# f32 parameter tables kept in DRAM, powers and weights made per channel quarter in that quarter's own Z buffer, two power tables, 112 quads instead of 107

## The chip, the core and the metric

The kernel runs on one core of a Trainium2 chip. The core has five engines, each with its own instruction stream: TensorE (PE, matmuls; PEld is its weight loads), VectorE (DVE), ScalarE (ACT), GpSimd (POOL) and SyncE (SP), whose queue issues nearly all DMAs here. The metric is the device time of one execution, in microseconds.

## The reference

The inputs are bf16: `x` (1 x 2048 x 512), attention weights, and the parameters of a diagonal state-space model with 512 channels and 128 complex states each.

```python
g = sigmoid((x * gate_w).sum(-1))
# branch a: attention, 32 heads of 16 channels, full softmax over 2048 keys
p = softmax(q @ k.T * 16 ** -0.5); a = (p @ v) @ wo
# branch b: y[l] = sum_m K[d, m] u[l - m], u = x
logdA = exp(log_dt) * (A_re + 1j * A_im)
K[d, l] = Re(sum_n C[d, n] * exp(logdA[d, n] * l) * dt * B[d, n])      # l = 0 .. 2047
b = causal_convolution(K, x) + x * Dskip
out = g * a + (1 - g) * b
```

The largest single job is the exponential: 32 heads x 2048 x 2048 scores, 134 million of them.

## The kernel before, in words

**Attention.** The work is cut into 2048 tiles of 128 keys x 512 queries for one head. A block is four heads with one of the four query chunks: there are 32, of 64 tiles each, and a quad is the four tiles of a block's four heads that share a key tile. A group takes three tiles: `qk(g)` writes their scores into one of two PSUM buffers of 3 x 512 columns (`SC0`, `SC1`), `ex(g)` (L987) makes one ACT exponential over 1536 columns into the ring `ET`/`EX`, and `pv` sums them against V into the PSUM bank `OA`, with a column of ones for the denominator. There are 683 groups.

**Quads on DVE and POOL.** Not all tiles go to ACT. `decide` (L865) may take a whole quad out: its four tiles become the third tile of four groups, whose ACT instruction then covers 1024 columns. For the third tile `bits` (L1010) has DVE write a 16-bit linear approximation of the exponential's bit pattern (`DZ`, L1014); when a quad's four tiles are there, `batch` has POOL make three shifted copies by an integer addition (`DU`, L1028, three per quad), and `sums` adds `DZ` and the three `DU` on TensorE. Before, 107 quads are handled so. `PACE` (L60) is a table of group number and number of quads that may have begun by then, `WIN` says which buffers are used in which groups.

**Kernel of the state-space branch.** `params` and `params2` (L1127, L1144) compute on DVE, in f32 and for all 512 channels at once, the powers L1, L2, ..., L64 of exp(logdA), the inverse powers M1 to M8, and the weights WW = C dt B and WN. From these, for each quarter of 128 channels:

- `powers` (L1221) makes 16 powers of each channel in a table `B16`, working in the f32 scratch `FP`;
- `weights` (L1181) makes the first 8 columns of `Z` in the same scratch;
- `zpart` (L1301) multiplies these out to the 32 columns of `Z`;
- `tables` makes, for each of a quarter's four channel blocks, the table `T` from `B16` and the digit table `DT` (four DVE products of 1536 columns at L1397, plus a copy by DMA);
- `kstage` (L1408) multiplies `T` by `Z` on TensorE into the PSUM bank `MB` and stores the block's kernel to DRAM (`kd`).

Before, `bases` (L1336) makes powers and weights of quarters 1, 2 and 3 ahead, in the staging buffers `B16s` and `Zbs`, and stores them to the DRAM scratch `bd`; quarter 0 is made in place once that is done (`TGO = 'bw31'`), and `tables` loads the other quarters back when their turn comes. There is one `B16` buffer (`NB = 1`) and two `Z` buffers (`NZ = 2`), used by the quarters in turn.

**Convolution and output.** `yloads` and `ystage` (L1503) convolve with Toeplitz slices of `kd` (`H`) and of x (`U`) on TensorE in `MB`, DVE scales and stores them (`Yst`, L1531), and `outs` (L1620) projects the attention with Wo, adds the convolution and writes the 16 row tiles of the output: 0 to 11 while attention runs, through `MB` and DVE (`fo`, L1652 and L1656), 12 to 15 after the last group.

**Fillers.** TensorE also multiplies a tile of zeros (`wm`) into a bank in use: L981 does it once in each even group, and the loop at L1812 adds as many as are needed for `FILL` units of array work per group.

**What sets the order.** The program is written out once, by a planner that runs when the kernel is built. The main loop (L1775) places each group's exponential and score matmuls; all else is threads with a priority, each a sequence of segments on one engine with a planned cost. `Sched.fill` picks the segment that could start first, then the one with the lower priority number. So constants such as `PACE`, `FILL`, `LAZY` or a priority change the order of the whole program. On the chip each engine runs its list in order and waits on semaphores.

## Time and profile before

| | us |
|---|---|
| median of 3 runs | 772.46 (772.38 to 777.15) |
| the profiled execution | 771.4 |
| its span in the profile | 769.6 |
| ACT busy | 745.3 (97%) |
| PE busy | 692.1 (90%) |
| DVE busy | 643.4 (84%) |
| POOL busy | 344.7 (45%) |

The durations below are those of the one profiled execution. Its own time is 1.8 us longer than its span, and 1.1 us under the median. In rows of groups of instructions the columns are: line, engine, operation, output<-input with shapes, count | busy us, mean ns of one | idle us of the engine before them and what ended it. Successive ACT instructions overlap by some 0.3 us in the records, so an ACT instruction's mean is longer than the distance between two starts.

### The profile page before, as it was taken

To read this page: it belongs to the slowest core of one execution; us is meant where nothing else is said; L and a number is where in the kernel's file an instruction comes from. 1 tells how busy PE (TensorE), PEld (TensorE's weight loads), DVE (VectorE), ACT (ScalarE), POOL (GpSimd) and SP (SyncE) were. 2 spreads that over 40 slices of the span, in tenths; PEclk is the share of its full clock that TensorE was granted. 3 is DMA by queue.
4 is the path that set the end of the run, shared out by engine and by line. 5 is a ranking of instruction groups with operands and counts; after the bars stand their busy time and mean duration, and the time that the engine had idled before them with its cause. 6 is when DMAs were issued, how large, how long until landed. Compare 5 with 4: busy or idle time off the path is not lost.

```text
span 769.6 us, 31882 instructions
## 1 busy us (share of the span) xinstructions
PE 692.1 (90%) x14179; PEld 291.5 (38%) x14180; DVE 643.4 (84%) x1069; ACT 745.3 (97%) x694; POOL 344.7 (45%) x340
## 2 busy tenths in 40 slices
PE   7777888787898899999999998999999999999996
PEld 3222332221344445443445444544443444422222
DVE  7999999999986998889998898877877566787883
ACT  7999999999999999999999999999999999999992
POOL 5000000010243464464655654545787555777771
PEclk9999999999999999999999999999999999999999
DMA  9459112212057665746645568356868999710001
GB/s 200 80 101 115 43 63 97 95 64 61 18 127 177 167 174 137 199 98 169 164 106 160 150 156 220 87 132 157 205 158 186 193 201 193 162 29 24 24 16 55
DMA packets 168427, 95.54 MB, mean 124 GB/s; under 512 B 117729, under 2 KB 148834, under 8 KB 167906
## 3 DMA queue, kind: packets, MB, share of 16 engines
q1 hardware_dynamic: 166274, 92.33, 51.4%
q8 instruction: 111, 1.82, 1.0%
q10 hardware_dynamic: 2016, 1.18, 0.7%
q14 instruction: 26, 0.21, 0.1%
HBM read 63.81 MB, written 19.42 MB: 108 GB/s over the span
## 4 chain that ended last, share of the span: by engine, by line
ACT 86%; PE 9%; DVE 2%; DMA 1%; issue 1%; ACTq 0%; POOL 0%; DVEq 0%
ACT ET L992 79%; ACT EX L992 7%; PE SC L734 4%; PE OA L734 3%; PE MB L734 2%; DMA Wk<-in_A_wqkv_dram 1%; DVE DZ L1014 1%; DVE T L1073 1%; DVE fo L1656 0%; ACTq L738 0%; DVE ft L1073 0%; DVE Z L1073 0%; POOL DU L1028 0%; ACT fo L1856 0%; DVE OT L1049 0%
## 5 line engine op out<-in xcount | busy, mean ns | idle before, releaser
L992 ACT ACTIVATE ET<-SC 128x1024 bf16<-128x1024 f32 (+1 forms) x615 | 679.5, 1380 | 4.0 <-PE SC L734 1.6
L1028 POOL INT64_ADD DU<-DZ x321 | 333.7, 1053 | 389.7 <-DVE B L1256 136.0
L1014 DVE TENSOR_SCALAR DZ<-SC 128x512 uint16<-128x512 f32 x428 | 287.5, 685 | 75.9 <-PE SC L734 70.9
L734 PE MATMUL SC<-Qm,KT 32*128 32x512 bf16 x2048 | 271.9, 384 | 59.9 <-ACT ET L992 54.0
L734 PEld LDWEIGHTS SC<-Qm,KT 32*128 32x128 bf16 x2048 | 69.5, 91 | 259.7 <-ACT ET L992 203.4
L734 PE MATMUL OA<-ET,VE 128*32 128x512 bf16 x1478 | 150.1, 387 | 1.7 <-DVE OT L1049 0.8
L734 PE MATMUL OA<-wm 32*128 32x512 bf16 (+3 forms) x721 | 148.7, 351 | 1.2 <-DVE idf L784 1.2
L734 PE MATMUL OA<-DU,VE 128*32 128x512 bf16 x1284 | 125.7, 386 | 0.6 <-POOL DU L1028 0.4
L734 PEld LDWEIGHTS MB<-U,H 128*32 128x32 bf16 x4096 | 85.7, 143 | 26.8 <-issue 14.9
L734 PE MATMUL MB<-U,H 128*32 128x128 bf16 (+7 forms) x4096 | 91.6, 224 | 0.6 <-DVE DZ L1014 0.6
L992 ACT ACTIVATE EX<-SC 128x1024 bf16<-128x1024 f32 (+1 forms) x68 | 73.0, 1290 | 0.0
L1073 DVE TENSOR_TENSOR T<-B,DT 128x1536 bf16<-128x1536 bf16 x64 | 65.3, 1054 | 0.0
L734 PEld LDWEIGHTS OA<-ET,VE 128*32 128x32 bf16 x1478 | 38.9, 95 | 59.9 <-issue 54.5
L734 PEld LDWEIGHTS OA<-DU,VE 128*32 128x32 bf16 x1284 | 34.0, 96 | 42.7 <-issue 34.2
L734 PEld LDWEIGHTS MB<-T,Z 128*32 128x32 bf16 x2048 | 44.6, 154 | 12.9 <-issue 8.8
L734 PE MATMUL MB<-T,Z 128*32 128x48 bf16 (+1 forms) x2048 | 48.4, 235 | 0.2 <-issue 0.2
L734 PE MATMUL OA<-DZ,VE 128*32 128x512 bf16 x428 | 42.3, 385 | 0.0
L734 PEld LDWEIGHTS OA<-wm 128*32 128x32 bf16 (+2 forms) x721 | 38.3, 94 | 10.5 <-issue 8.3
L1531 DVE TENSOR_TENSOR Yst<-MB,gt 128x512 bf16<-128x512 f32 x32 | 22.0, 686 | 18.4 <-PE MB L734 17.9
L1049 DVE STREAM_TRANSPOSE OT<-OA 128x512 f32<-128x512 f32 x32 | 22.7, 709 | 3.0 <-PE OA L734 3.0
L1073 DVE TENSOR_TENSOR ft<-Z,DM 128x1024 bf16<-128x1024 bf16 x32 | 23.6, 756 | 0.0
L734 PE MATMUL MB<-Wv,xT 128*32 128x128 bf16 x1024 | 19.9, 220 | 0.7 <-DVE VE L838 0.5
(143 smaller groups left out, 438.1 us busy)
## 6 DMA issues: line engine op xcount, KB each, us to landing
H<-gm_kd SPq DMA_DIRECT2D x128, 256.0 KB, 4.0
U<-gm_xs SPq DMA_DIRECT2D x128, 134.2 KB, 3.8
T<-B SPq DMA_DIRECT2D x16, 256.0 KB, 2.9
gm_yd<-Yst SPq DMA_DIRECT2D x64, 64.0 KB, 2.9
gm_bd<-B16s SPq DMA_DIRECT2D x3, 1024.0 KB, 4.9
B<-gm_bd SPq DMA_DIRECT2D x12, 256.0 KB, 3.6
gm_kd<-Ks SPq DMA_DIRECT2D x64, 40.0 KB, 2.6
gm_xs<-xP SPq DMA_DIRECT2D x16, 136.0 KB, 7.3
```

What stands on the lines that cost most here:

```text
L734: op("PE", lambda t: t.matmul(out(), lhsT(), rhs(), start=start, stop=stop, skip_group_check=True, **kw), R, W, c=c, lat=.15, a=a, cfg=cfg)
L992: op("ACT", lambda a: a.activation(E(at, [[1, 512 * n]]), sc(0, [[1, 512 * n]]), AF.Exp, scale=DH ** -0.5), [(sc, i, g) for i in range(n)] ...
L1014: op("DVE", lambda v: v.tensor_scalar(z.u16(512 * k, [[1, 512]]), sc(1024, [[1, 512]]), XS, XB, ALU.mult, ALU.add), [(sc, 2, g)], [(z, k, ...
L1028: op("POOL", lambda v, u=u, cut=cut: v.int64_add(u.u64(), z.u64(), cut * 0x0001000100010001), R, [(u, 0, i)], c=1.016, lat=.09, lk=True)
L1049: op("DVE", lambda v: v.transpose(OT(512 * w, [[1, 512]]), OA(0, [[1, 512]])), [(OA, 0, b)], [(OT, w, b)], c=.64)
L1073: op(eng, lambda v: v.tensor_tensor(o(), a(), b_(), f), R, W, c=c)
L1531: op("DVE", lambda v, w=w, h=h: v.tensor_tensor(Yst(1024 * w + 4 * h, [[128, R8], [8, 16], [1, 4]]), MB(0, [[1, R8], [R8, 16], [NC, 4]]), ...
```

## The change

The f32 results `L1, L2, L4, L8, M2, M4, WW, WN` are stored to a DRAM scratch `pd`, laid out by quarter (`park`, 16 DMAs of 256 KB). `ploads` loads a quarter's eight tables into that quarter's Z buffer, seen as f32 (4 DMAs per quarter, 1 MB in all), once the Z buffer's earlier quarter is done with (`KT3`, `KT7`). `powers` and `weights` then work inside the Z buffer, with its later bf16 columns as their scratch; `zpart` writes over them last. The scratch `FP`, the staging buffers and the way through `bd` go, and so do the 20 copies into `FP`. There are two `B16` buffers. `DT` is split by quarter, so `short` for the three digit tables becomes `digit`: 24 instructions for 6. The thread that made the tables is split into `bases` (powers, weights, `zpart`) and `tables` (`T`).

With that go new planner constants: a new `PACE`, other waits for starting threads (`XGO`, `TGO`), `outs` at priority 1 in place of 6, and `ZEND = 230`: from group 230 on no filler matmuls are issued. In the program as built 112 quads are taken instead of 107, the fillers `OA<-wm` of 128 columns by 512 fall from 313 to 117, those of 32 by 512 from 172 to 72.

```diff
-LAZY = 9
-PDEL = .2
+LAZY = 8
+PDEL = 0.1
+ZEND = 230
+OUTP = 1
-OVER = .3
+OVER = 0.4
-PACE = ((0, 0), (110, 0), (170, 4.8), (230, 16.2), (300, 28.8), (370, 42.8), (440, 54.0), (510, 70.1), (560, 79.1), (620, 93.5), (683, 108.6))
+PACE = ((0, 0), (40, 0), (90, 0.0), (140, 0.0), (200, 9.0), (270, 24.4), (340, 41.2), (420, 58.8), (500, 74.8), (570, 88.8), (630, 102.6), (683, 112.67))
-XGO = 'g14'
+XGO = 'g30'
-TGO = 'bw31'
-BPR = 2
-KP = 0.20
-NB = 1
+TGO = 'g0'
+TP = 2
+KP = 0.4
+NB = 2
...
-    sb("DT", 3 * 6 * D)
+    for k in range(4):
+        sb(f"DT{k}", 3 * 6 * P)
-    sb("FP", 2 * 128 * 8, FP32)
-    sb("B16s", 2 * 128 * 16)
-    sb("Zbs", 2 * 128 * 8)
...
-            if i == 0 and n == 3 and g % 2 == 0 and sch.now is not None:
+            if i == 0 and n == 3 and g % 2 == 0 and g < ZEND and sch.now is not None:
...
+    def digit(n):
+        m, x = DIGITS.index(n), B[n]
+        for qr in range(4):
+            d = B[f"DT{qr}"]
+            yield ("DVE", .45)
+            op("DVE", lambda v, d=d, qr=qr: v.tensor_copy(d(6 * P * m, [[2 * P, 2], [2, P], [1, 2]]), x(P * qr, [[D, 2], [1, P], [0, 2]])), [(x, 0)], [(d, (m, 0))], c=.07 + .28)
+            op("DVE", lambda v, d=d, qr=qr: v.tensor_scalar(d(6 * P * m + 4 * P, [[2, P], [1, 2]]), x(D + P * qr, [[1, P], [0, 2]]), -1.0, None, ALU.mult), [(x, 0)], [(d, (m, 1))], c=.07 + .14)
+        sch.mark("D" + n)
...
-        for l, n in enumerate(("WW", "WN")):
-            yield ("DVE", .25)
-            op("DVE", lambda v, l=l, n=n: v.tensor_copy(FP(128 * l, [[e8, 2], [1, 128]]), B[n](d0, [[D, 2], [1, 128]])), key(n), rw(l), c=.25)
...
-        yield from copy(1, "L1")
-        yield from copy(2, "L2")
-        yield from copy(4, "L4")
...
+    def park():
+        for n in ("L1", "L2", "L4", "L8", "M2", "M4", "WW", "WN"):
+            yield ("AFTER", n)
+            k = PDS.index(n)
+            for h in range(2):
+                yield ("SP", .6)
+                dma("SP", lambda e, k=k, n=n, h=h: e.dma_start(pd.dram(1024 * h + 128 * k, [[8192, P], [2048, 4], [1, 128]]), B[n](D * h, [[128, 4], [1, 128]])),
+                    key(n), [(pd, (n, h))], c=.6, lat=4, b=.65)
+        sch.mark("pd")
+
+    def ploads():
+        yield ("AFTER", "pd")
+        for qr in range(4):
+            Z = B[f"Z{qr % NZ}"]
+            if qr >= NZ:
+                yield ("AFTER", f"KT{4 * (qr - NZ) + 3}")
+            for k0, n, over, at in ((0, 2, [3, 5], 256), (2, 2, [(1, 0), (1, 1)], 640), (4, 1, [(0, 0), (0, 1)], 1024), (5, 3, [(2, 0), (2, 1)], 1536)):
+                yield ("SP", .6)
...
+    def bases():
         yield ("AFTER", TGO)
         for qr in range(4):
+            if qr >= NB:
+                yield ("AFTER", f"T{4 * (qr - NB) + 3}")
+            yield from powers(qr, B16, [(B16, 0), (B16, 2)])
+            yield from weights(qr)
             yield ("AFTER", "DM9")
             yield from zpart(qr)
+            sch.mark(f"ba{qr}")
...
-                   (tables(), 2), (bases(), BPR), (xrows(), 4), (outs(), 6)):
+                   (tables(), TP), (bases(), 2), (park(), 2), (ploads(), 2), (xrows(), 4), (outs(), OUTP)):
...
-        sch.fill(t, t + OVER, want)
-        lack = want - p.act
+        sch.fill(t, t + OVER, want if g < ZEND else 0)
+        lack = want - p.act if g < ZEND else 0
```

How the order moves is shown at three places.

**The end, on TensorE.** From the last two score tiles (`SC<-Qm,KT` x2, group 682) up to the output projection of tiles 13 to 15. `OA<-DU` and `OA<-DZ` are the sums of the last quads, `OA<-ET` and `OA<-EX` those of ACT's tiles, `MB<-Wo,OnR` with the two `MB<-Yl` one output tile of the first twelve, `MB<-Wo,OnT` tile 12. Before:

```order
L734 MATMUL SC<-Qm,KT 128x512 x2
L734 MATMUL OA<-DZ_65,VE 32x512 x4
L734 MATMUL MB<-Wo,OnR_75 32x512 x8
...
L734 MATMUL OA<-DU_70,VE 32x512 x4
L734 MATMUL MB<-Yl,idb 32x512 x4
L734 MATMUL MB<-Yl_102,idb 32x512 x4
L734 MATMUL OA<-DU_71,VE 32x512 x4
L734 MATMUL MB<-Wo,OnR_75 32x512 x16
...
L734 MATMUL MB<-Wo,OnT_72 32x512 x12
```

Now:

```order
L740 MATMUL OA<-DZ_62,VE 32x512 x4
L740 MATMUL MB<-Wo,OnR_75 32x512 x8
L740 MATMUL MB<-Yl,idb 32x512 x4
L740 MATMUL SC<-Qm,KT 128x512 x2
L740 MATMUL OA<-ET,VE 32x512 x4
L740 MATMUL OA<-DU_66,VE 32x512 x4
L740 MATMUL MB<-Yl_102,idb 32x512 x4
L740 MATMUL OA<-DU_67,VE 32x512 x4
L740 MATMUL OA<-ET,VE 32x512 x4
L740 MATMUL OA<-DU_68,VE 32x512 x4
L740 MATMUL MB<-Wo,OnT_72 32x512 x12
```

Before, output tiles 9, 10 and 11 stand behind the last score tiles (the shown lines of 8 and 16 and, among those left out, 4, 4 and another 16); now only the last step of tile 11 does, the second `Yl`. The last quad has moved up as well: its last DZ is read ahead of the last score tiles, not behind.

**The end, on DVE.** From the last quad's conversions (`DZ`) on; `CAST fo<-MB` is the evacuation of one output tile, `OT<-OA` the transpose of a finished block. Before:

```order
L1014 TENSOR_SCALAR DZ_64<-SC 128x512 x4
L1014 TENSOR_SCALAR DZ_65<-SC 128x512 x4
L1656 CAST fo<-MB 128x512 x4
L1049 STREAM_TRANSPOSE OT<-OA 128x512
L1057 RECIPROCAL Rz<-OT 128x16
```

Now:

```order
L1070 TENSOR_TENSOR ON<-OT,Rz 128x16x16
L1671 CAST fo<-MB 128x512
L1020 TENSOR_SCALAR DZ_62<-SC 128x512 x3
L1671 CAST fo<-MB 128x512
L1020 TENSOR_SCALAR DZ_62<-SC 128x512
L1671 CAST fo<-MB 128x512
L1055 STREAM_TRANSPOSE OT<-OA 128x512
```

Before, four evacuations stand behind the last conversion; now one.

**The quarters' powers, on DVE.** A stretch of quarter 2's part, which before stands ahead of the first conversion of a quad (`FP` scratch, staging buffer `B16s`):

```order
L1206 COPY FP<-WN 128x2x128
L829 CAST KT<-MB 128x512
L1073 TENSOR_TENSOR ft_146<-FP,M_134 128x512
L1073 TENSOR_TENSOR ft_147<-FP,M_134 128x512
L1189 CAST Zbs<-FP 128x256
L1073 TENSOR_TENSOR FP<-ft_146,ft_147 128x256
```

Now a like stretch for quarter 3, near the end of its weights, in the Z buffer itself:

```order
L1218 CAST Z_153<-Z_153 128x256
L1079 TENSOR_TENSOR Z_153<-ft_148,ft_149 128x512
L1020 TENSOR_SCALAR DZ_56<-SC 128x512
L1079 TENSOR_TENSOR Z_153<-ft_148,ft_149 128x512
L1546 TENSOR_TENSOR Yst<-MB,gt 128x128x4
L1020 TENSOR_SCALAR DZ_56<-SC 128x512 x2
```

Before, the powers and weights of quarters 1, 2 and 3 and most of quarter 0's powers stand ahead of the first conversion. Now those of quarters 0 and 1 do, with about half of quarter 2's powers; the rest of quarter 2 and quarter 3 stand between the quads. Ahead of the first conversion stand now also the `zpart` of quarters 0 and 1, 29 of the 64 products for `T` and the transposes and casts of six of the sixteen `kstage`; before, none of these. In all DVE has 297 instructions ahead of it before and 357 now. The first conversion belongs to group 112 before, to group 141 now.

## The prediction

> **What bounds the kernel now.** I read the page first: which engine is full, and which one the chain of work that ended last runs through.

> ```profile
> span 769.6 us, 31882 instructions
> PE 692.1 (90%) x14179; PEld 291.5 (38%) x14180; DVE 643.4 (84%) x1069; ACT 745.3 (97%) x694; POOL 344.7 (45%) x340
> PEclk9999999999999999999999999999999999999999
> ACT 86%; PE 9%; DVE 2%; DMA 1%; issue 1%; ACTq 0%; POOL 0%; DVEq 0%
> ```

> ACT works 97% of the span and is 86% of the chain, so a change pays by what it takes off ACT, or off the stretches in which ACT has nothing to do. The groups by form say what one exponential costs, ACT's waits how long it stood still between them.

> ```profile
> L992 ACT ACTIVATE ET<-SC 128x1024 bf16<-128x1024 f32 x367 | 356.2, 1184 | 2.1 <-PE SC L734 1.3
> L992 ACT ACTIVATE ET<-SC 128x1536 bf16<-128x1536 f32 x248 | 346.0, 1672 | 1.9 <-PE OA L734 1.5 <-PE SC L734 0.4
> ACT ET L992 <- PE SC L734: 1.6, 5, 0.5
> ACT ET L992 <- PE OA L734: 1.5, 2, 1.3
> ```

> Busy time by count is 346.0/248 = 1.395 us for the wide form and 356.2/367 = 0.971 us for the narrow one: 0.424 us for 512 columns. (The means 1672 and 1184 ns overlap their neighbours; busy time counts overlap once.) Between the exponentials ACT lost only 1.6 + 1.5 = 3.1 us. Its one large gap is at the end, so I read the timeline there, engine by engine.

> ```profile
> 749.74 3.78 ACT L992 ACTIVATE EX<-SC 128x1024 bf16<-128x1024 f32 x3
> 765.27 1.07 ACT L1856 CAST fo<-SC 128x512 bf16<-128x512 f32 x2 [11.75 <-PE SC L734]
> 749.76 0.69 DVE L1014 TENSOR_SCALAR DZ<-SC 128x512 uint16<-128x512 f32 x1 [0.23 <-PE SC L734]
> 750.37 0.68 DVE L1656 CAST fo<-MB 128x512 bf16<-128x512 f32 x1
> 753.96 0.69 DVE L1656 CAST fo<-MB 128x512 bf16<-128x512 f32 x1 [2.91 <-PE MB L734]
> 758.87 0.69 DVE L1656 CAST fo<-MB 128x512 bf16<-128x512 f32 x1 [1.76 <-PE MB L734]
> 754.80 1.05 PE L734 MATMUL MB<-Wo,OnR 128*32 128x512 bf16 x16 [0.52 <-DVE fo L1656]
> 755.66 0.65 PE L734 MATMUL MB<-Yl,idb 128*32 128x512 bf16 x8
> 759.62 0.83 PE L734 MATMUL MB<-Wo,OnT 128*32 128x512 bf16 x12 [0.86 <-DVE fo L1656]
> 761.09 0.59 PE L734 MATMUL SC<-Wo,OnT 128*128 128x512 bf16 x2 [0.16 <-issue]
> 761.61 0.40 PE L734 MATMUL OA<-EX,VE 128*32 128x512 bf16 x4
> ```

> The exponentials end at 765.27 - 11.75 = 753.5. The sums over the last of them (`OA<-EX`) start at 761.61, 8.1 us later: PE first builds output tiles 9, 10 and 11, each of which needs the one bank `MB` and so waits for DVE's evacuation of the tile before. From 761.61 to the end of the span it is 8.0 us, a chain of small steps that the change leaves alone.

> **The change part by part.**

> *Five quads more.* Each takes four tiles from ACT: 20 x 0.424 = 8.5 us off an engine that hardly waits. DVE and POOL pay:

> ```profile
> L1014 DVE TENSOR_SCALAR DZ<-SC 128x512 uint16<-128x512 f32 x428 | 287.5, 685 | 75.9 <-PE SC L734 70.9 <-PE OA L734 2.1 <-POOL DU L1028 1.5
> L1028 POOL INT64_ADD DU<-DZ x321 | 333.7, 1053 | 389.7 <-DVE B L1256 136.0
> L1234 DVE COPY FP<-L 128x256 f32<-128x256 f32 x12 | 3.4, 282 | 0.0
> L1120 DVE CAST DT<-L 128x2048 bf16<-128x2048 f32 x3 | 3.6, 1217 | 0.0
> L1124 DVE TENSOR_SCALAR DT<-L 128x1024 bf16<-128x1024 f32 x3 | 2.0, 682 | 0.0
> L1120 DVE CAST DL<-L 128x512 bf16<-128x512 f32 x1 | 0.4, 421 | 0.0
> ```

> DVE gets 20 x 287.5/428 = 13.4 us, POOL 15 x 1.053 = 15.8 us. The 20 copies into `FP`, each of 256 columns, save 20 x 0.282 = 5.6 us. The digit tables took 3.6 + 2.0 = 5.6 us; now 12 casts at `DL`'s 0.421 and 12 products of 256 columns at the copy's 0.282 make 8.4, so +2.8. DVE is left with 13.4 - 5.6 + 2.8 = +10.6: 654 us of a span of some 756, 87%. POOL comes to 344.7 + 15.8 = 361, under half. Neither becomes the bound on the whole.

> *Does DVE fit stage by stage?* Work moves ahead of the first conversion, and ACT cannot pass a conversion that is late: its third tile holds the score bank that the group after next needs.

> ```profile
> 20.00:160.00 140.00, 111.53 (x2179) 40.25 (x2171) 134.30 (x254) 140.00 (x107) 1.20 (x5) 1.00 0.43 86
> 160.00:760.00 600.00, 559.18 (x11748) 242.01 (x11748) 490.01 (x772) 589.80 (x574) 333.65 (x321) 1.00 0.55 131
> L1014 DVE TENSOR_SCALAR DZ<-SC x428: 626/691/847, 162.5 to 749.8; 128x512 uint16<-128x512 f32 x143
> L1073 DVE TENSOR_TENSOR T<-B,DT 128x1536 bf16<-128x1536 bf16 x64 | 65.3, 1054 | 0.0
> L1073 DVE TENSOR_TENSOR ft<-Z,DM 128x1024 bf16<-128x1024 bf16 x32 | 23.6, 756 | 0.0
> L1437 DVE STREAM_TRANSPOSE Kt<-MB 128x512 f32<-128x512 f32 x16 | 11.4, 711 | 4.5 <-PE MB L734 4.4
> L1440 DVE CAST Ks<-Kt 128x512 bf16<-128x512 f32 x16 | 7.3, 455 | 0.5
> ```

> (The windows' columns are length, then busy of PE, PEld, DVE, ACT, POOL, then the granted clock.) Up to the first conversion, at 162.5, DVE is nearly full: 134.3 of 140 us. Ahead of it now stand 29 `T` products (29 x 65.3/64 = 29.6), 36 of `zpart` (36 x 0.756 = 27.2), six blocks' `Kt` with their three casts (6 x (0.711 + 0.455) = 7.0, and the 12 small casts at the copy's 0.282 at most 3.4), four evacuations more at 0.69 (2.8) and the digits' 2.8. Against that, 33 instructions of powers and weights fewer, by the window's mean of 134.30/254 = 0.529 us, are -17.5, and 18 of the copies -5.1: together +50.2 by durations. Durations overlap: the conversion at 749.76 lasts 0.69, its successor starts 0.61 later. For 60 instructions more that is 60 x 0.08 = 4.8 less, +45. The first conversion belongs to a group 29 later; the wide form's 1.395 makes 40.5 us of that, and 5.7 us were idle: 46. It just fits, with some 5 us of error either way; 5 us too late costs ACT 5 us, once. After it DVE has 490.0 + 10.6 - 45 = 456 us in 600 - 40.5 - 14 = 545, 84%, beside 490.0 of 600, 82%, before.

> I take the waits between exponentials from 3.1 to 4.1 us, **+1.0**. The bounds are -3.1 (all gone) and +10: 5 at the front, and 5 where a conversion stands behind a f32 power of quarters 2 or 3.

> Those powers read two SBUF inputs beside POOL's additions, where before they stood ahead of them. The `T` products already did: 65.3/64 = 1.02 us each beside POOL, 0.07 from the mean that overlap leaves, so the row holds the price of it, and I add nothing.

> [...]

> *The way through DRAM.* Sixteen stores of 256 KB and sixteen loads on SP's queue take the place of 6 and 18.

> ```profile
> gm_bd<-B16s SPq DMA_DIRECT2D x3, 1024.0 KB, 4.9
> 29.22 11.11 SPq L1464 DMA_TRANSPOSE xP<-in_A_x_dram  x8
> 46.23 3.07 SPq L848 DMA_DIRECT2D Qm<-gm_qd  x4
> 58.64 0.68 DVE L1073 TENSOR_TENSOR WN<-pt,pt 128x512 f32<-128x512 f32 x1
> 74.89 1.22 DVE L1120 CAST DT<-L 128x2048 bf16<-128x2048 f32 x1
> ```

> An issue takes 3.07/4 = 0.77 us, a transpose 11.11/8 = 1.4. The sixteen stores are 12 us of SP ahead of what it did there: the transposes of x, which only the convolution reads, and the `Qm` loads for the third block, which starts near 70 (43 groups of 1.395 after a start near 12), 20 us after they were made. The last store waits for `WN`, done at 59.3. Even with all seven transposes that stand near it behind that, the two stores and the first three loads are issued by 59.3 + 9.8 + 3.9 = 73 and land 4.9 later, by 78. The first power that reads them stands behind the last digit cast and its product, which begin at 74.89 before and end near 78 with the digits' 2.8. So it is just hidden; without that, DVE idles and it is the late front above. Quarters 2 and 3 load when `KT3` and `KT7` free their buffer; behind the waiting load on SP is the very `Ks` store that follows the same block, so no one else waits. I put it at nothing.

> *The end.* On PE only the second `Yl` of tile 11 stands behind the last score tiles; tile 12's Wo can start about when the exponentials end. From there to the last sums it is 761.61 - 759.62 = 2.0 us by the rows above: 8.1 - 2.0 = **6.1 us** less. Bounds: 0, if evacuations still chain behind the last conversions, and 7.6, if tile 12 is done by then and only its last 0.5 is left. The three tiles' matmuls do not vanish; they move in among the score matmuls, 3 x (1.05 + 0.65) = 5 us, hidden by PE's waits for ACT:

> ```profile
> PE SC L734 <- ACT ET L992: 59.1, 175, 1.0
> 282.00:740.00 458.00, 436.83 (x9320) 192.08 (x9311) 371.41 (x583) 455.01 (x453) 279.72 (x272) 1.00 0.60 142
> 282.00:740.00 458.00, 80.64 (x275) 19.64 (x275) 0.00 (x0) 1.00 0.60 142
> ```

> *No fillers from group 230.* The first window is all work from there on, the second the zero products `wm` alone: 80.6 of PE's 436.8 us go, and PE is left with 356/458 = 78%. On the path they are nothing, since PE waits for ACT anyway. What they might hold up is the clock, a rival below.

> **Sum.** 771.4 - 8.5 - 6.1 + 1.0 = 757.8 for the profiled execution; the median of the runs is 1.1 above it: **759.0**.

> **The rivals.**

> *Half the gain is eaten.* The plan is dense: DVE at 83 to 87% in order, PE with output steps between score matmuls. If the front is late by the full 5 and mid conversions by 5 (+10 in place of +1), it is 768. If only the end stays as it was, 765. For: the front fits with nothing to spare. Against: 3.1 us of waits in a plan that was as dense. 762 to 771.

> *Waits vanish.* With -3.1 and 7.6 at the end: 771.4 - 8.5 - 7.6 - 3.1 + 1.1 = 753. Little in the trace asks for it.

> *The clock falls, slower.* Without `wm`, PE idles shortly after every group, from about 310 us to the end. How far the clock would go down no row shows; I take a half. Then its 0.78 us per us of ACT's work becomes 1.56, and 0.56 us is lost per us. From 759 it takes 21 us of loss to be slower by over 1%, 38 us at half clock, a twelfth of the stretch; a fifth of it, 92 us, would give 810. Against: PE stood waiting for ACT 175 times for up to 1.0 us, and PEclk is 9 in every slice, though with `wm` filling in. How it goes without, no row shows.

> [...]

> **How the numbers follow.** The forecast (753 to 762) gets 0.62, half eaten 0.24, waits vanish 0.06, the clock 0.08. One per cent, about what a measurement here can tell, is 764.7 and 780.2. Faster: 0.62 + 0.06 and a quarter of the half-eaten case, 0.74; slower: the clock and 0.01 of backlog beyond the bounds, 0.09; within: 0.17. The range 752 to 769 leaves out the clock, 0.04 below and 0.05 of the half-eaten case.

> **What would show it.** ACT busy near 737 and waits of its exponentials near 4 us; `OA<-EX` 2 us after the last exponential; DVE busy near 654; first conversion near 201; PEclk 9 after 310. Wrong: a long idle of ACT before 201 (front), PEclk under 9 (clock), idles behind `fo` at the end.

## The result and the profile after

The changed kernel takes 761.79 us (median of 4 runs, 760.5 to 762.85) against 772.6: ratio 0.9845, 95% interval 0.9806 to 0.9885. Measured once more beside the kernel before, in experiment 9, it was 762.02 against 775.19: 0.9832 (0.9805 to 0.9859). The forecast was 759.0, the range 752 to 769. The profiled execution took 761.73 us, 9.7 less than that of before. Ratios leave out executions over 1.5% above the shortest of their kernel; that concerns two of the five in experiment 12, the profiled one among them.

The page of the changed kernel, its first lines and the chain that ended last:

```profile
span 759.9 us, 31256 instructions
PE 686.0 (90%) x13835; PEld 288.6 (38%) x13836; DVE 650.3 (86%) x1087; ACT 738.6 (97%) x694; POOL 361.0 (48%) x355
PEclk9999999999999999999999999999999999899999
ACT 75%; PE 14%; DVE 4%; DMA 3%; POOL 2%; SPq 1%; issue 1%; ACTq 0%; DVEq 0%
```

DVE at 650.3 and POOL at 361.0 are what the sum had (654 and 361). PE's busy time falls by only 6 us, though the fillers' own busy time, 80 us of it after 282 us, is gone but for 2.5: their records lie over those of other matmuls. Leaving the records of `wm` out of the trace of before, those of the other matmuls still cover 432.8 of the 458 us. PEclk has an 8 in one slice. ACT by form, and its waits:

```profile
L998 ACT ACTIVATE ET<-SC 128x1024 bf16<-128x1024 f32 x395 | 379.3, 1143 | 5.0 <-PE SC L740 3.3
L998 ACT ACTIVATE ET<-SC 128x1536 bf16<-128x1536 f32 x223 | 308.9, 1676 | 0.5 <-PE SC L740 0.5
ACT ET L998 <- PE SC L740: 3.9, 12, 0.5
ACT EX L998 <- PE SC L740: 0.9, 1, 0.9
ACT ge L1591 <- DMA gp<-gm_gld: 0.6, 1, 0.6
```

The waits are 3.9 + 0.9 + 0.6 = 5.4 us where 4.1 was forecast. But the idle column hides most of what ACT loses: the record of a narrow exponential lasts about 1.18 us and the next one starts 0.904 us after it when nothing is late, so a delay shows as idle only beyond the first 0.28 us. I therefore counted both traces by starts: each of the 682 steps from one exponential's start to the next, less the usual step (0.904 us after a narrow form, 1.330 after a wide one, the medians in both traces). That gives this ledger of the profiled executions, in us:

| | usual steps | stretched by | last exponential ends | from there to the end |
|---|---|---|---|---|
| before | 724.7 | 15.3 | 753.5 | 16.1 |
| changed | 716.2 | 20.2 | 749.3 | 10.6 |
| difference | -8.5 | +4.9 | -4.2 | -5.5 |

(The first exponential starts 0.3 earlier and the last one's record is 0.3 shorter, which closes the sum.) So the slots gave 8.5 as forecast, the end 5.5 for a forecast of 6.1, and the stretching took back 4.9, for a forecast of 1.0. Of the 4.9, 2.4 lie between 640 and 680 us, 2.4 between 400 and 480, 1.3 between 80 and 120, and the other slices together have 1.2 less. The end, in the timelines of ACT, DVE and PE:

```profile
747.97 1.31 ACT L998 ACTIVATE EX<-SC 128x1024 bf16<-128x1024 f32 x1
754.75 1.30 ACT L1871 CAST fo<-SC 128x512 bf16<-128x512 f32 x2 [5.46 <-PE SC L740]
748.36 0.69 DVE L1671 CAST fo<-MB 128x512 bf16<-128x512 f32 x1 [3.14 <-PE MB L740]
749.10 0.83 PE L740 MATMUL MB<-Wo,OnT 128*32 128x512 bf16 x12
751.11 0.39 PE L740 MATMUL OA<-EX,VE 128*32 128x512 bf16 x2
```

One evacuation is left behind the last conversion, tile 12's Wo starts at 749.10, and the last sums at 751.11, 1.8 us after the last exponential (749.28), where it was 8.1.

### The stages on DVE and POOL, and the clock

The conversions by tile, then groups by form of DVE and POOL:

```profile
L1020 DVE TENSOR_SCALAR DZ<-SC x448: 628/691/902, 201.7 to 744.5; 128x512 uint16<-128x512 f32 x150
L1020 DVE TENSOR_SCALAR DZ<-SC 128x512 uint16<-128x512 f32 x448 | 299.7, 686 | 82.9 <-PE SC L740 71.3 <-POOL DU L1034 7.9 <-PE OA L740 1.4
L1034 POOL INT64_ADD DU<-DZ x336 | 348.5, 1051 | 344.7 <-DVE B L1287 157.9
L1079 DVE TENSOR_TENSOR T<-B,DT 128x1536 bf16<-128x1536 bf16 x64 | 62.3, 1009 | 0.0
L1079 DVE TENSOR_TENSOR ft<-Z 128x1024 f32<-128x1024 f32 x16 | 19.5, 1250 | 0.0
```

The first conversion comes at 201.7; 162.5 + 40.5 = 203 was its due time, so DVE did fit ahead of it, and ACT was stretched by 3.0 us up to 200 us against 2.2 before. Conversions now wait 7.9 us for POOL's additions to free a buffer, 1.5 before; one of these waits ends at 460.1, and the stretching by 0.8 at 459 is there. The f32 powers show little of a price beside POOL: of the 16 products of 1024 columns seven run after the first conversion, and five of these took 1208 to 1235 ns, as those ahead of it did (1214 to 1251), two 1418 and 1494: half a microsecond in all. With the smaller f32 products and sums of the powers and weights, 26 in all behind the first conversion, it comes to some 0.9 us.

The largest stretching lies between 640 and 680 us. That window, and PE in it:

```profile
640.00:680.00 40.00, 38.67 (x688) 14.67 (x684) 30.06 (x47) 37.60 (x41) 25.84 (x26) 0.91 0.57 140
645.57 1.20 PE L740 MATMUL SC<-Qm,KT 32*128 32x512 bf16 x4 [0.26 <-DVE DZ L1020]
647.06 0.89 PE L740 MATMUL MB<-U,H 128*32 128x128 bf16 x32 [0.29 <-DMA H<-gm_kd]
647.88 0.61 PE L740 MATMUL SC<-Qm,KT 32*128 32x512 bf16 x3
```

The mean granted clock of the window is 0.91 of full. The clock's records have it at half for 6.83 us from 646.2; the score matmuls just behind take 0.61 us where they took 0.39. Before has no such stretch until its last microseconds (from 768.4 on).

### The profile page after: what moved, and what is told of

Same layout as the page of the kernel before. It is cut to its first block, busy times and chain, and to the rows that moved or that the text cites. A ratio compares the mean times of both kernels' runs of the same rounds, so it can differ in the third digit from the quotient of the medians.

```text
span 759.9 us, 31256 instructions
## 1 busy us (share of the span) xinstructions
PE 686.0 (90%) x13835; PEld 288.6 (38%) x13836; DVE 650.3 (86%) x1087; ACT 738.6 (97%) x694; POOL 361.0 (48%) x355
## 3 DMA queue, kind: packets, MB, share of 16 engines
q10 hardware_dynamic: 2016, 1.18, 0.7%
## 4 chain that ended last, share of the span: by engine, by line
ACT 75%; PE 14%; DVE 4%; DMA 3%; POOL 2%; SPq 1%; issue 1%; ACTq 0%; DVEq 0%
ACT ET L998 68%; ACT EX L998 7%; PE SC L740 6%; PE OA L740 5%; PE MB L740 3%; DVE DZ L1020 2%; POOL DU L1034 2%; DMA H<-gm_kd 1%; DMA Wk<-in_A_wqkv_dram 1%; DMA gp<-gm_gld 0%; DVE T L1079 0%; DVE ft L1079 0%; DVE ON L1070 0%; SPq L1558 0%; DVE OT L1055 0%
## 5 line engine op out<-in xcount | busy, mean ns | idle before, releaser
L998 ACT ACTIVATE ET<-SC 128x1024 bf16<-128x1024 f32 (+1 forms) x618 | 672.7, 1335 | 5.6 <-PE SC L740 3.9
L1034 POOL INT64_ADD DU<-DZ x336 | 348.5, 1051 | 344.7 <-DVE B L1287 157.9
L1020 DVE TENSOR_SCALAR DZ<-SC 128x512 uint16<-128x512 f32 x448 | 299.7, 686 | 82.9 <-PE SC L740 71.3
L740 PE MATMUL SC<-Qm,KT 32*128 32x512 bf16 x2048 | 275.8, 386 | 58.3 <-ACT ET L998 52.6
L740 PE MATMUL OA<-DU,VE 128*32 128x512 bf16 x1344 | 129.4, 386 | 2.0 <-POOL DU L1034 1.8
L1079 DVE TENSOR_TENSOR T<-B,DT 128x1536 bf16<-128x1536 bf16 x64 | 62.3, 1009 | 0.0
L740 PE MATMUL OA<-wm 128*32 128x256 bf16 (+3 forms) x349 | 60.6, 338 | 1.2 <-DVE idf L790 1.2
L740 PE MATMUL MB<-T,Z 128*32 128x64 bf16 (+1 forms) x2048 | 45.5, 235 | 0.1
L1079 DVE TENSOR_TENSOR ft<-Z 128x512 f32<-128x512 f32 (+3 forms) x48 | 38.7, 831 | 0.3
L1079 DVE TENSOR_TENSOR Z<-ft,ft 128x1024 bf16<-128x1024 bf16 (+3 forms) x56 | 31.7, 566 | 0.6
## 6 DMA issues: line engine op xcount, KB each, us to landing
gm_xs<-xP SPq DMA_DIRECT2D x16, 136.0 KB, 4.9
```

Source lines behind the costliest of these rows:

```text
L740: op("PE", lambda t: t.matmul(out(), lhsT(), rhs(), start=start, stop=stop, skip_group_check=True, **kw), R, W, c=c, lat=.15, a=a, cfg=cfg)
L998: op("ACT", lambda a: a.activation(E(at, [[1, 512 * n]]), sc(0, [[1, 512 * n]]), AF.Exp, scale=DH ** -0.5), [(sc, i, g) for i in range(n)] ...
L1020: op("DVE", lambda v: v.tensor_scalar(z.u16(512 * k, [[1, 512]]), sc(1024, [[1, 512]]), XS, XB, ALU.mult, ALU.add), [(sc, 2, g)], [(z, k, ...
L1034: op("POOL", lambda v, u=u, cut=cut: v.int64_add(u.u64(), z.u64(), cut * 0x0001000100010001), R, [(u, 0, i)], c=1.016, lat=.09, lk=True)
L1079: op(eng, lambda v: v.tensor_tensor(o(), a(), b_(), f), R, W, c=c)
```

## The experiments

My theory after the comparison: 8.5 for slots, 5.5 at the end, 5 lost; half of the loss because the output steps, now at priority 1, put their loads ahead of those of `H` on SP, so that PE idles without fillers and the clock falls. The rivals are in the expectations.

**1. Output steps back at priority 6.**

```diff
-OUTP = 1
+OUTP = 6
```

> The changed kernel with the output steps back at priority 6. Theory: the changed kernel is 11 us faster as 8.5 (20 slots off ACT) plus 5.5 (end) less 5 of new waits, and half of these come from the output steps' loads standing ahead of the loads of H on SP's queue, which leaves TensorE idle without fillers and halves its clock for 6.8 us near 646. Then this run loses the 5.5 at the end and gets some 2.4 back: about 765, last sums 7 to 8 us after the last exponential, and no half clock before the end. Rival: the clock falls because the fillers are gone, whatever the priority of the output steps: about 767, with a half-clock episode somewhere.

Measured: 759.83 us (757.42 to 763.38), ratio 0.9824 (0.9784 to 0.9865). The convolution's last scaling, and ACT's idle at the end:

```profile
L1546 DVE TENSOR_TENSOR Yst<-MB,gt x32: 672/686/693, 234.3 to 658.6; 128x512 bf16<-128x512 f32 x32
ACT fo L1871 <- PE SC L740: 4.1, 1, 4.1
```

The convolution ends at 658.6, against 673.7 with priority 1, and the end shrinks further, to 9.3 us, instead of going back. So both theory and rival missed on the end: the priority did not shorten it.

**2. Fillers in all groups.**

```diff
-ZEND = 230
+ZEND = 683
```

> The changed kernel with fillers in every group up to the end. Theory: the H loads are still late, but the fillers hold the array's use, so the clock stays full, and the 2.4 us of the episode come back: about 759.5. Rival: on a TensorE this full the fillers push score tiles back, and the waits of ACT between exponentials grow instead: 764 or more.

Measured: 767.55 us, ratio 0.9917 (0.989 to 0.9944), 5.6 us slower than the changed kernel by the two ratios.

```profile
core 0: 763.5 us, clock 0.999
L1546 DVE TENSOR_TENSOR Yst<-MB,gt x32: 653/682/692, 233.3 to 691.3; 128x512 bf16<-128x512 f32 x32
ACT fo L1871 <- PE SC L740: 12.4, 1, 12.4
```

The clock stays full, as the theory had it, and the last exponential ends at 745.9, 3.4 earlier than in the changed kernel. But the convolution ends 18 us later, at 691.3, and the end grows from 10.6 to 17.6. The size was right for the rival, the place was neither's: the convolution comes later, not the score tiles. The written order has it so already: the convolution's last matmul stands 53 groups ahead of the last score tiles with fillers and 75 without. So it is the planner that gives the fillers the places of the convolution; whether PE on the chip had no room for both, this run does not show.

**3. 107 quads.** The table's numbers scaled by 107.6/112.67.

```diff
-PACE = ((0, 0), (40, 0), (90, 0.0), (140, 0.0), (200, 9.0), (270, 24.4), (340, 41.2), (420, 58.8), (500, 74.8), (570, 88.8), (630, 102.6), (683, 112.67))
+PACE = ((0, 0.0), (40, 0.0), (90, 0.0), (140, 0.0), (200, 8.6), (270, 23.3), (340, 39.35), (420, 56.15), (500, 71.43), (570, 84.8), (630, 97.98), (683, 107.6))
```

> The changed kernel with its table scaled to 107 quads. Theory: 20 slots are worth 8.5 us, less some 1.5 of conversions that wait for POOL only because there are more of them: 768 to 769. Rival: the quads' gain is mostly eaten by crowding, so taking them away costs little: 764 or less.

Measured: 767.59 us, ratio 0.9915 (0.989 to 0.9941): 5.4 us slower than the changed kernel by the two ratios (6.4 by the ratio of experiment 9; the intervals leave some 3.5 either way), between theory and rival. By starts the usual steps are 724.7 again, exactly 8.5 more. The end is 9.3, and its profiled execution has 20 us at half clock in four pieces.

**4. The kernel before with output steps at priority 1.**

```diff
-                   (tables(), 2), (bases(), BPR), (xrows(), 4), (outs(), 6)):
+                   (tables(), 2), (bases(), BPR), (xrows(), 4), (outs(), 1)):
```

> The kernel before with the output steps at priority 1, nothing else. Theory: the end alone, 5.5 to 6.1 us less: about 767, last sums about 2 us after the last exponential; with its fillers the clock stays full. Rival: the steps moved in among the score tiles cost ACT as much as they save at the end: 770 to 773.

Measured: 774.77 us, ratio 1.0009 (0.9996 to 1.0022).

```profile
L1531 DVE TENSOR_TENSOR Yst<-MB,gt x32: 671/691/693, 233.6 to 687.2; 128x512 bf16<-128x512 f32 x32
ACT fo L1856 <- PE SC L734: 13.5, 1, 13.5
```

The convolution ends 12 us later (687.2 for 675.2) and the end is longer. The theory fell; nothing is gained, as the rival had it, but it is the end that grew and not the score tiles that slipped. The code says why the two go together: no output tile starts before the last block's convolution is stored (`yr` marks ahead of the loop in `outs`). I formed another: **the end is a chain**, convolution done, then twelve output tiles through one bank; those that do not fit before the last exponential are paid at the end, by my estimate then some 2.4 us each (the table below makes it some 2.1 from nine tiles to twelve). What the order shows, how many groups stand behind the last convolution matmul and how many tiles behind the last score tiles, should then foretell the end.

**5. The kernel before without fillers from group 230.** The same three conditions as in the change's diff, on the kernel before.

```diff
-        sch.fill(t, t + OVER, want)
-        lack = want - p.act
+        sch.fill(t, t + OVER, want if g < 230 else 0)
+        lack = want - p.act if g < 230 else 0
```

> The kernel before without fillers from group 230 on, nothing else. Theory now: the end is set by a chain, convolution done, then twelve output tiles one after the other through the bank MB, and what does not fit before the last exponential is left for the end. In this program's order the convolution ends 81 groups before the last score tiles, as before (82), and 2.75 output tiles stand behind them (3 before): so the end stays and nothing is gained, 0 to -1 us against the kernel before; half-clock episodes would add 1 to 4. Rival: fillers cost TensorE time that ACT waits for, as 767.5 against 761.8 in the changed kernel suggests; then it is 5 us faster than before here as well.

Measured: 773.69 us, ratio 0.9989 (0.9964 to 1.0014): nothing gained.

```profile
core 0: 772.3 us, clock 0.995
L1531 DVE TENSOR_TENSOR Yst<-MB,gt x32: 653/691/692, 233.5 to 679.6; 128x512 bf16<-128x512 f32 x32
ACT fo L1856 <- PE SC L734: 11.5, 1, 11.5
```

The end is 15.8, as the chain foretold. Here the written order leaves the convolution where it was (81 groups ahead of the last score tiles, 82 before), so the places of the fillers give nothing.

**6. The kernel before with 112 quads and no fillers from 230.** `PACE` of the changed kernel, and the edit of experiment 5.

> The kernel before, its powers and its way through bd kept, with the changed kernel's table for 112 quads and no fillers from group 230. Theory: the 20 slots come without the parked tables, -8.5; 2.75 output tiles still stand behind the last score tiles, so the end stays at some 16 us: 8 us faster than before, and 5 slower than the changed kernel with outputs at priority 6. Rival: without the parked tables the old layout cannot feed 112 quads, ACT's waits grow by the gain: 0 to 3 us faster than before.

Measured: 769.29 us, ratio 0.9927 (0.9896 to 0.9957), 5.6 us faster than before and 6.3 slower than the changed kernel.

```profile
ACT ET L992 <- PE SC L734: 6.4, 16, 0.7
L1531 DVE TENSOR_TENSOR Yst<-MB,gt x32: 674/681/693, 223.8 to 691.3; 128x512 bf16<-128x512 f32 x32
ACT fo L1856 <- PE SC L734: 11.3, 1, 11.3
```

The slots come (usual steps 716.2), 7.0 us of stretching eats most of them (22.3 for 15.3), and the end stays at 15.6. The time lies between theory and rival. The old layout carries 112 quads, but its convolution ends 16 us later than before. What the rest of the change brings is the end: 15.6 against 10.6. That rest is the parked tables, the second power table, `KP` and the other planner constants together; experiments 11 and 12 take two of these apart, and no run has the parked tables alone.

**7. No fillers at all after the start.**

```diff
-ZEND = 230
+ZEND = 0
```

> The changed kernel without any filler after the start. Its array use ahead of the first conversions is the lowest of the kernel. Theory (clock): the granted clock drops to half in episodes of 3.4 to 6.8 us there; each us at half clock costs about 0.5 us, so mean clock 0.97 to 0.98 and 8 to 12 us more than the changed kernel, 770 to 774. Rival: the fillers hold nothing up, clock 0.995 and 760 to 763.

Measured: 768.87 us, ratio 0.9934 (0.991 to 0.9958).

```profile
core 0: 764.7 us, clock 0.980
PEclk9998999999999999999999999899999999999999
ACT ET L998 <- PE SC L740: 8.3, 20, 1.3
```

Every run had a mean clock between 0.971 and 0.983; the theory's clock came, and its time came near, though only one of the stretches lies ahead of the first conversion, where the theory put them. There are seven stretches of half clock, 27 us without the last. The price can be read from all runs, since the clock's records read full or half (1 and 0.5 before and in the changed kernel), and a mean clock c over a span s then means 2 x (1 - c) x s at half clock: over these ten runs the time rises by some 0.2 us per us at half clock, over the runs of the kernel before by 0.26, 0.41 and 0.31 (16, 28 and 11 runs on three chips). One pair of traces is too few for it: here the last exponential ends 4.0 us later than in the changed kernel's first trace for 20 us more at half, but in the changed kernel's second (experiment 9, 13.7 us at half) it ends as late.

**8. 117 quads, output steps at priority 6.** The table scaled by 117.67/112.67, and `OUTP = 6`.

> The changed kernel with 117 quads and the output steps at priority 6. Theory (output chain): the exponentials end some 8 us earlier than in the changed kernel with outputs at 6, at 739; but its convolution ends only 30 groups before the last score tiles and eight output tiles stand behind them, 8 x 2.4 = 19 us at the end: about 769. Rival: the exponentials set the time, 752 to 755.

Measured: 773.11 us, ratio 0.999 (0.9958 to 1.0021).

```profile
L1546 DVE TENSOR_TENSOR Yst<-MB,gt x32: 652/682/693, 233.6 to 713.1; 128x512 bf16<-128x512 f32 x32
ACT fo L1871 <- PE SC L740: 28.6, 1, 28.6
```

The exponentials do end earlier, at 743.8, and the whole gain is lost behind them: the convolution ends at 713.1, and ACT idles 28.6 us.

**9 and 10. The changed kernel and the one of experiment 1, side by side.**

> The changed kernel itself once more, on the same chip as the next run. Theory and rival alike: about 762, mean clock 0.992 to 0.996; it is the reference for the next three.

> The changed kernel with the output steps at priority 6, beside the changed kernel on one chip. Theory (output chain): the output steps' loads and matmuls no longer stand ahead of the convolution, which ends some 15 us earlier (658.6 against 673.7), so the twelve output tiles are done before the last exponential and ACT meets less of them: 2 to 3 us faster than the changed kernel. Rival: the difference between the two runs so far was the chips' and the clock's, and side by side they are within 1 us.

Measured on the same chip: 762.02 (759.86 to 766.17) and 762.57 (759.66 to 765.7), both at ratio 0.9832. The rival holds: the priority of the output steps moves the convolution's end from 678.1 to 663.2 and the end from 10.6 to 9.3, and no difference in time is left above the spread. The part of my theory on SP's queue falls with it: the run at priority 6 has a half-clock stretch too, at 650.4. No version tried beats the changed kernel for certain.

Both traces also show what the late load of the gate can set off. ACT waits for `gp` (2.0 and 1.4 us; 1.7 in experiment 11), PE waits for ACT in turn (2.7 us in experiment 9), and at 87 to 89 us the clock goes to half for 3.4 us in all three. In the first trace of the changed kernel, with 0.6 us of wait, it stays full there.

**11. KP back to 0.20** (with priority 6).

```diff
-KP = 0.4
+KP = 0.20
```

> As the run before, with the one planner constant KP, the priority of the kstage threads, back from 0.4 to the 0.20 of the kernel before. Theory (output chain): in this program's order the convolution ends 59 groups before the last score tiles in place of 88, and 2.75 output tiles stand behind them in place of none: 2.75 x 2.4 = 6.6 us more at the end, 765 to 767. Rival: what counts is the layout in DRAM and the quads, not the order of the convolution; then it stays within 2 us of the run before.

Measured: 765.71 us, ratio 0.9878 (0.9847 to 0.991), 3.1 more than experiment 10 beside it, which is what the theory had; the two intervals just overlap.

```profile
L1546 DVE TENSOR_TENSOR Yst<-MB,gt x32: 667/681/693, 249.1 to 688.5; 128x512 bf16<-128x512 f32 x32
ACT fo L1871 <- PE SC L740: 11.5, 1, 11.5
```

One planner constant brings the old end back: convolution done at 688.5 for 663.2, 16.7 us from the last exponential to the end for 9.3. The last exponential itself comes 3.0 us earlier, which is why the time grows by less than the end. The written order has nine tiles ahead of the last score tiles here and twelve in experiment 10.

**12. One power table** (with priority 6).

```diff
-NB = 2
+NB = 1
```

> As the run before last, with one power table in place of two (NB = 1), so a quarter's powers wait until the last T of the quarter before is made. Theory (output chain): the order has the convolution end 22 groups before the last score tiles and nine output tiles behind them: 9 x 2.4 = 22 us more at the end, less 2 for the chain that is shorter by then: 777 to 782, slower than the kernel before. Rival: the second table changes only when DVE does its work, which has room: 760 to 764.

Measured: 790.58 us (788.48 to 801.22; the ratio's three runs 788.48 to 790.58), ratio 1.0168 (1.0135 to 1.02): slower than the kernel before. The lines are of the profiled execution of 801.2 us.

```profile
core 0: 799.4 us, clock 0.951
L1546 DVE TENSOR_TENSOR Yst<-MB,gt x32: 652/688/693, 213.8 to 736.2; 128x512 bf16<-128x512 f32 x32
ACT fo L1871 <- PE SC L740: 31.8, 1, 31.8
```

The convolution ends at 736.2; ACT then idles 31.8 us. The sign is the theory's, and nine tiles stand behind the last score tiles as it said; the size is more, and some of it is the clock, at half for 20.5 us from 769.6 in this execution. The stretching is 33.5 us too, and what that owes to the late powers no run separates. Within this plan the second power table is worth more than the five quads.

Over all kernels, in the order of the convolution's end (us, profiled executions):

| kernel | last `Yst` | tiles begun by the last exponential | end, after the last exponential | ratio to before |
|---|---|---|---|---|
| 1: priority 6 | 658.6 | 12 | 9.3 | 0.9824 |
| changed | 673.7 | 12 | 10.6 | 0.9845 |
| before | 675.2 | 9 | 16.1 | 1 |
| 7: no fillers at all | 677.7 | 12 | 11.4 | 0.9934 |
| 5: before, no fillers | 679.6 | 9 | 15.8 | 0.9989 |
| 3: 107 quads | 682.7 | 12 | 9.3 | 0.9915 |
| 4: before, priority 1 | 687.2 | 9 | 17.8 | 1.0009 |
| 11: KP | 688.5 | 9 | 16.7 | 0.9878 |
| 2: fillers | 691.3 | 9 | 17.6 | 0.9917 |
| 6: before, 112 quads | 691.3 | 9 | 15.6 | 0.9927 |
| 8: 117 quads | 713.1 | 5 | 33.9 | 0.9990 |
| 12: one table | 736.2 | 3 | 37.4 | 1.0168 |

(A tile counts as begun when its `fo` evacuation on DVE has started.) The end follows the tiles: twelve leave 9.3 to 11.4 us, nine 15.6 to 17.8, five and three 33.9 and 37.4. The convolution's end alone does not tell it: in experiment 3 it comes 7.5 us later than before, and still all twelve tiles fit. What counts besides is how fast tiles follow one another. From the first evacuation to the ninth a tile takes 7.3 us before and 5.1 in the changed kernel. The fillers do not make that difference: without them the old kernel still takes 6.8 (experiment 5), and the changed one takes 5.0 with them (experiment 2). Between experiments 5 and 6 only `PACE` differs, and there it goes from 6.8 to 5.1; but the convolution ends 12 us later with the new table, and the end stays. The old table has 55 conversions in the last 60 groups, the new one 47, which may be why; no run tests it.

## Why the prediction was right

- **Five quads, 8.5 us.** Right to the tenth in the steps by starts (724.7 to 716.2), and again in experiment 3. As time the quads were worth 5.4, or 6.4 by experiment 9's ratio: less than their slots, part of it clock, since experiment 3's runs have means of 0.985 to 0.994 and the changed kernel's 0.992 to 0.996.
- **DVE stage by stage.** Right: first conversion at 201.7, busy 650.3 for 654, and no late front. For the moved powers beside POOL I had added nothing; by the products above they took half a microsecond longer in the large ones and some 0.9 in all.
- **The way through DRAM, at nothing.** Nearly: the gate's load `gp` lands later (3.3 us after its issue at 80.7; before, 1.6 after 79.0), and ACT, not DVE, waits for it (0.6 us in the changed kernel, 2.0 in experiment 9); by starts the step across it is 1.45 us longer than usual. The step asked who stands behind the stores on SP, and left out the gate.
- **The end, 6.1 us.** Right in size (5.5), and experiments 4, 9 and 10 show that the new priority is not what does it. Without the second power table (12), the new KP (11) or the end of the fillers (2) it is gone, so these are needed together; the new `PACE` alone does not bring it (6). `LAZY`, `PDEL`, `OVER`, `XGO` and `TGO` were not tried one by one.
- **No fillers, "on the path they are nothing".** This step failed, though the time came out. The 78% to which it put PE does not exist: busy times of groups that overlap cannot be subtracted. In the same window of the changed kernel PE is busy 439.4 of 458 us (96%) with 2.5 us of `wm` left in it:

```profile
282.00:740.00 458.00, 439.40 (x8617) 183.62 (x8621) 376.21 (x607) 452.24 (x461) 309.77 (x301) 0.99 0.51 127
282.00:740.00 458.00, 2.54 (x10) 0.65 (x10) 0.00 (x0) 0.99 0.51 127
```

  Fillers in the changed kernel cost 5.6 us (experiment 2), in the kernel before nothing (experiment 5). The cost is in the written order, where they put the convolution 22 groups later: I asked whether ACT waits for PE, and not what else on PE ends late. The forecast kept its size because the end, which held this gain, was priced from the finished order.
- **Waits between exponentials, +1.0.** The mis-sized term: +4.9 by starts, +2.3 by the idle rows. Both its size and its measure were off; 15.3 us of stretching were there before, where I read 3.1. It is most of the difference between 757.8 and 761.7.
- **The clock, as rival.** It came in small: half clock for 6.8 us and 2.4 us lost in that slice, 0.35 us per us. Over the runs of experiment 7 and of the kernel before it is 0.2 to 0.4, where I had put 0.56. The half that I took for the fallen clock is what the records have (0.5 over the 6.83 us from 646.2).

What stays open: what the parked tables do without the second power table and the new constants; why the changed kernel's stretching differs between executions (20.2 in one, 23.9 in experiment 9), beyond the clock's part of it, and how much of the 2.4 us between 400 and 480 is POOL's buffers.

## What to carry to other kernels

A stall should be counted from start to start: when records overlap, the idle column shows only what exceeds the overlap (0.28 us here). Busy times of groups whose records overlap cannot be subtracted from an engine's total: here 78 us of fillers went from one window, and PE's busy time over the span fell by 6. An engine that waits for the bounding engine may still carry a second chain that ends late; ask when each chain ends, not only who waits for whom. And a plan's gain can hang on one constant far from the edit: here one power table fewer turned 1.7% faster (experiment 10) into 1.7% slower (experiment 12).

## What was unexpected of the hardware

What went ahead of these stretches can be counted in part. I took the array's use in each beat from the starts of the matmul records in nine executions, from 20 to 730 us. Use is rows x columns of the array, times columns moved; 512 columns count 0.215 us, the distance at which whole-array matmuls of 512 columns start one after another in the trace of before, near 10 us. 21 beats were followed by half clock, some 1810 at full clock were not. Each beat with a use under 0.31 was followed by half clock, 16 of the 21 drops had 0.31 or less before them, five 0.35 to 0.41. Above 0.31 the use alone does not decide: some 110 beats between 0.31 and 0.41 kept the clock. In the changed kernel the beat ahead of 646.18 had 0.35, and another with 0.35, from 192.2, kept it. If the same matmuls are spread over the length of their records, the line is less sharp (12 drops lie under the lowest beat that kept the clock), so 0.31 holds for this way of counting and these nine executions. The idles were mostly short: in 15 of the 21 beats PE's longest wait was 0.75 us or less, in three it was 1.0 to 1.3, and in the three behind the late gate 2.1 within the beat. The same place can have half clock in one execution and full in another: in experiment 1 the use was 0.25 over 3.4 us from 642.5, across two beats, and the clock stayed; in experiment 10, the same program, it fell at 650.4. That it hangs on how the beat falls is my reading of these two. At 0.2 to 0.4 us for each us at half clock that is a part of the 2 to 8 us by which executions of one kernel mostly differ (2.4 in the changed kernel's four, 6.3 in experiment 9, 8.4 in experiment 8).
